# Two token chunks share the first projection block, and the final flag is loaded inside the schedule

## The chip, the cores and the metric

The kernel runs on one core of one Trainium2 chip. The metric is device time in microseconds (us) of one execution of the program. The engines are named as in the profile: PE (TensorE, matmuls; PEld its weight loads), DVE (VectorE), ACT (ScalarE), POOL (GpSimd) and SP (SyncE, which issues the DMAs here).

## The reference

Two computations on tokens of 2048 x 448 are written side by side into one output. A is a Fourier mixing layer with given DFT matrices, B is softmax attention with 16 heads of 28 columns:

```python
a = einsum("bsd,ed->bse", x, dft_hid_re); b = einsum("bsd,ed->bse", x, dft_hid_im)
A = einsum("ts,bse->bte", dft_seq_re, a) - einsum("ts,bse->bte", dft_seq_im, b)
q, k, v = split_heads(x @ wqkv)            # 16 heads, 28 columns each
B = merge_heads(softmax(q @ k.T * 28**-0.5) @ v) @ wo
return concatenate([A, B], -1)
```

All of it is float32. The kernel keeps the precision by splitting each operand into a high part in a reduced format and a low rest, and by adding three products (high x high, low x high, high x low).

## The kernel before, in words

**The order.** Nothing in the program says in which order an engine runs its instructions. Each step is a task with an engine, a due key, a duration and the tasks that it depends on; a planner (`Schedule.run`) plays the schedule through on the host, before the kernel is built, and puts into each engine's queue whichever ready task has the lowest key. On the chip each queue then runs strictly in that order and waits by semaphores. The planner models DMAs by a flow: each transfer occupies `size / FLOW` us after time 20 (`FLOW_IN` before), sizes in KB, and lands a fixed lag later (lines 68 and 278 to 293). A wrong figure there doesn't make the result wrong, but puts instructions at places where they wait. `P_H`, `fkey` and the like are due times worked out ahead.

**The start.** `FirstWeights` loads the weights of the first three column blocks of wqkv (384 columns) in four quarters of the contraction, w0 to w3 (192 KB each). `load_x` loads a chunk of 512 tokens, also in four quarters (256 KB each): x00 to x03 for chunk 0, x10 to x13 for chunk 1. ACT makes the high part of each (L560 for weights, L490 for tokens), DVE or POOL the low part (L427). Keys put SP's queue in the order w0, x00, w1, x01, w2, x02, w3, x03, x10, x11 and on. Until the first operands are there, `warm` (L920) runs `N_WARM` = 7 matmuls on ones.

`first_chunk` then multiplies chunk 0 with the three weight blocks a quarter at a time (33 matmuls, L616): the first quarter needs w0 and x00 only. Chunks 1 to 3 follow by `project`, one block after the other through `chain` (L581). `stored` evicts a finished bank: ACT copies the high part (L597), DVE subtracts for the low part (L598), and two stores of 256 KB each put them into DRAM (qkd, L600 and L601).

**The stretch from 37 to 84 us.** PE computes the values (`values`, 16 blocks of 11 matmuls of 448 columns, again by L581); for each block DVE copies the bank (L671 to L673) and SP stores it in a layout by heads (vd, L675: runs of 32 numbers). Between them SP loads rows of q and k from qkd (L745 and L746, 112 and 56 KB, a pair for each tile) and pieces of further weights (`Piece`: load L523, ACT's high part L524, POOL's low part L530, and small parts L539 and L542).

Attention of a head begins with `first_tiles`: for each of four query tiles a score matmul (L806), then ACT saves the scores (L810) and DVE transposes and reduces them (L811, L812). When all four are through, DVE forms a maximum for each query (L818 to L823). For each tile in turn DVE then transposes it back (L832) into a tile `mb`, of which there is one; DVE or POOL copies a row of it into q (L835); POOL or DVE adds it to the saved scores (L837), and ACT takes the exponential (L839). The score matmuls proper (L865) need the row in q, ACT evicts them with an exponential (L869), and runs of 8 or 10 groups of four L848 matmuls multiply with v. To fill PE, the planner weaves in projections of later heads (L581) and the Fourier part: `hidden`, then `sequence` (L718), which streams the DFT matrices through `Piece`.

**The end.** The output projection (L1003, stored by L1011) runs among the last `sequence` blocks; the last block is added to the first half by DVE (L736) and stored (L738). DVE has written a flag `fi` (whether all sums and values lay in a safe range); `values_load` (L1027) has every engine load it into a register and check it, and a branch that is not taken here (`tc.If`) would repeat the attention in another way. L1128 is the end of the program.

## Time and profile before

| | us |
|---|---|
| median of 3 runs | 1010.61 (1010.15 to 1011.03) |
| the profiled execution | 1010.71 |
| its span in the profile | 1008.9 |
| PE busy | 1001.6 |
| ACT busy | 712.3 |
| POOL busy | 366.9 |
| DVE busy | 319.8 |

The profiled execution is 1.8 us longer than the span, which goes from the first to the last recorded instruction. The granted TensorE clock was 1.00. In a timeline a row holds the start, the duration, the engine, the line, the operation with out<-in, and in brackets the idle time of the engine before it with the one that ended it. A row with x3 joins three like instructions in a row. In the view of waits a row holds who waited for whom, the sum, how often, and the longest. Matmuls overlap, so their durations add up to more than the time from start to start. Lines are those of the kernel before; below `first_chunk` the changed kernel's lines are one higher.

### The profile page before, as it was taken

The numbers are of one execution on the slowest core, as the hardware profiler recorded it, in microseconds if no ns is written. First come the engines' busy times: TensorE is split into PE (matmuls) and PEld (weight loads), VectorE is DVE, ScalarE is ACT, GpSimd is POOL, SyncE is SP. The second block draws the span as 40 slices with busy tenths as digits, with TensorE's granted clock in tenths as the row PEclk, the third lists the DMA queues.
The fourth block names the chain that finished last, engine by engine and source line by source line (L and its number), as shares of the span: only waits on it lengthen the run. The fifth ranks groups of instructions, "written<-read, shape, count | busy, mean of one in ns | idle before, by whom it ended". The sixth has DMA issues, their size and how long they took to land.

```text
span 1008.9 us, 15993 instructions
## 1 busy us (share of the span) xinstructions
PE 1001.6 (99%) x5634; PEld 735.3 (73%) x5634; DVE 319.8 (32%) x608; ACT 712.3 (71%) x1410; POOL 366.9 (36%) x338
## 2 busy tenths in 40 slices
PE   8999999999999999999999999999999999999998
PEld 7896667777766876686668667766786677667797
DVE  6362525251515042412314051614042152300112
ACT  6117979788767866796679778877786687668242
POOL 5112234353324323442325443434334252444530
PEclk9999999999999999999999999999999999999999
DMA  9797464323233333333233424332433343233463
GB/s 327 226 163 205 127 188 150 98 76 114 69 102 102 112 96 106 97 106 102 80 111 110 132 71 119 93 112 80 148 98 100 117 141 105 70 123 117 139 187 130
DMA packets 109908, 124.84 MB, mean 124 GB/s; under 512 B 48640, under 2 KB 61440, under 8 KB 109824
## 3 DMA queue, kind: packets, MB, share of 16 engines
q1 hardware_dynamic: 109824, 123.78, 40.8%
q8 instruction: 45, 0.74, 0.3%
q14 instruction: 39, 0.32, 0.1%
HBM read 89.92 MB, written 33.69 MB: 123 GB/s over the span
## 4 chain that ended last, share of the span: by engine, by line
PE 98%; DVE 1%; DMA 1%; SPq 0%; issue 0%; DVEq 0%
PE bank L718 31%; PE bank L865 23%; PE bank L848 22%; PE bank L581 17%; PE bank L1003 4%; PE bank L806 1%; DMA kept<-xb 1%; DVE big L427 0%; SPq L488 0%; SPq L559 0%; DVE kept L598 0%; DVE kept L736 0%; DVEq L427 0%
## 5 line engine op out<-in xcount | busy, mean ns | idle before, releaser
L869 ACT ACTIVATE kept<-bank 128x512 f32<-128x512 f32 x944 | 509.4, 673 | 90.7 <-PE bank L865 87.6
L530 POOL TENSOR_TENSOR wlo<-wraw,whi 128x512 fp32r<-128x512 f32 (+1 forms) x164 | 202.9, 1237 | 471.4 <-ACT whi L524 397.1
L865 PE MATMUL bank<-q,k 98*128 98x512 f32 x960 | 329.4, 398 | 0.0
L718 PE MATMUL bank<-big,whi 128*128 128x448 f32 x1024 | 310.9, 367 | 0.0
L848 PE MATMUL bank<-kept,v 128*32 128x512 f32 x2016 | 224.4, 593 | 0.0
L718 PEld LDWEIGHTS bank<-big,whi 128*128 128x128 f32 x1024 | 193.3, 189 | 29.2 <-issue 3.4
L865 PEld LDWEIGHTS bank<-q,k 98*128 98x128 f32 x960 | 180.4, 188 | 44.2 <-issue 11.7
L718 PE MATMUL bank<-big,wlo 128*128 128x448 f32 x512 | 188.3, 368 | 0.0
L848 PEld LDWEIGHTS bank<-kept,v 128*32 128x32 f32 x2016 | 63.5, 110 | 144.4 <-issue 142.3
L524 ACT ACTIVATE whi<-wraw 128x512 fp32r<-128x512 f32 x164 | 113.8, 694 | 21.0 <-PE bank L718 17.0
L718 PEld LDWEIGHTS bank<-big,wlo 128*128 128x128 f32 x512 | 96.7, 189 | 16.9 <-issue 5.9
L837 POOL TENSOR_TENSOR kept<-kept,mb 128x512 f32<-128x512 f32 x54 | 79.5, 1473 | 62.9 <-DVE mb L832 27.5
L581 PE MATMUL bank<-wd,whi 128*128 128x448 f32 x256 | 79.8, 367 | 0.0
L811 DVE STREAM_TRANSPOSE mb<-bank 128x512 f32<-128x512 f32 x64 | 45.8, 715 | 101.6 <-PE bank L806 87.9
L839 ACT ACTIVATE kept<-kept 128x512 f32<-128x512 f32 x64 | 45.1, 772 | 33.3 <-POOL kept L837 29.9
L581 PE MATMUL bank<-big,whi 128*128 128x512 f32 x175 | 60.1, 394 | 0.2 <-DVE kept L598 0.2
L832 DVE STREAM_TRANSPOSE mb<-am 128x512 f32<-128x512 f32 x64 | 45.4, 710 | 41.1 <-POOL kept L837 39.9
L810 ACT ACTIVATE kept<-bank 128x512 f32<-128x512 f32 x64 | 41.6, 672 | 22.5 <-PE bank L806 21.6
L581 PEld LDWEIGHTS bank<-wd,whi 128*128 128x128 f32 x256 | 48.3, 189 | 6.1 <-issue 0.8
L894 ACT ACTIVATE kept<-bank 128x512 f32<-128x512 f32 x16 | 9.5, 597 | 55.1 <-PE bank L848 55.1
L776 DVE TENSOR_REDUCE ok<-v 128x1 f32<-128x512 f32 x16 | 11.0, 686 | 115.5 <-DMA v<-vd 115.4
L736 DVE TENSOR_TENSOR kept<-bank,kept 128x448 f32<-128x448 f32 x15 | 9.3, 623 | 120.2 <-PE bank L718 106.0
(74 smaller groups left out, 745.8 us busy)
## 6 DMA issues: line engine op xcount, KB each, us to landing
wraw<-wre SPq DMA_DIRECT2D x64, 256.0 KB
wraw<-wim SPq DMA_DIRECT2D x64, 256.0 KB
qkd<-kept SPq DMA_DIRECT2D x40, 256.0 KB
wraw<-xa SPq DMA_DIRECT2D x32, 256.0 KB
k<-qkd SPq DMA_DIRECT2D x64, 112.0 KB
q<-qkd SPq DMA_DIRECT2D x64, 112.0 KB
out<-kept SPq DMA_DIRECT2D x31, 224.0 KB
kept<-xb SPq DMA_DIRECT2D x16, 256.0 KB
```

The costliest lines, as they stand in the source:

```text
L524: a = act(key + (0 if early else 1), lambda: nc.scalar.activation(self.hi.t, raw.t, AF.Copy), ACT_S, soon=SOON, deps=[ld], acq=[self.hi], ...
L530: b = sch.add(e, at, lambda g: eng[g].tensor_tensor(self.lo.t[:, :n], raw.t[:, :n], f32(self.hi.t)[:, :n], op=ALU.subtract), deps=[a], acq ...
L581: nc.tensor.matmul(o.t[:, :cols], w(), x(), start=(i == 0), stop=(i == n - 1))
L718: nc.tensor.matmul(o.t[:, :D], a.t[:, k, :], b[:, q * 4 + k, :], start=(q == 0 and k == 0 and j == 0), stop=(q == 3 and k == 3 and j == 2))
L810: made.append(act(key, lambda o=o, s=s: nc.scalar.activation(s.t, o.t, AF.Copy), deps=[m], use=[o, s.pair], lock=[o]))
L811: t = dve(key, lambda o=o, tm=tm: nc.vector.transpose(tm.t, o.t), 0.73, deps=[m], acq=[tm], use=[o], lock=[o], own=RAW_S)
L832: t = dve(key, lambda mb=mb, c=c: nc.vector.transpose(mb.t, f32(am.t)[:, c * NT:(c + 1) * NT].unsqueeze(2).to_broadcast([P, NT, 32])), 0.7 ...
L837: sh = sch.add({"DVE": 0.8, "POOL": POOL_2}, key, lambda e, s=s, mb=mb: eng[e].tensor_tensor(s.t, s.t, mb.t, op=ALU.add), deps=[t, made[c] ...
L839: shown.append(act(key, lambda s=s: nc.scalar.activation(s.t, s.t, AF.Exp, scale=SCALE), ACT_S, deps=[sh], use=[s.pair]))
L848: nc.tensor.matmul(o.t[c * VW:(c + 1) * VW, :], VT[h].t[:, kt // 4, kt % 4, :], tiles[c].t, start=(kt == 0), stop=(kt == NT - 1))
L865: m = pe(key, lambda e, o=o, q=q, kt=kt: nc.tensor.matmul(o.t, KT[h][kt // 4].t[:KM, kt % 4 * P:(kt % 4 + 1) * P], q.t[:KM, :], start=True ...
L869: es[h, kt].append(act(key - 20, lambda o=o, p=p: nc.scalar.activation(p.t, o.t, AF.Exp, scale=SCALE), deps=[m], use=[o, p.pair]))
```

## The change

Four things are changed.

1. `first_chunk` becomes `first_chunks`, for chunks 0 and 1: for each quarter of the contraction first the matmuls of chunk 0 and then those of chunk 1, 66 in all. They hold six banks until the end. `project` does the rest from chunk 2 on. The key of chunk 1's loads is moved so that each of its quarters stands in SP's queue right behind that of chunk 0: w0, x00, x10, w1, x01, x11 and on.
2. `N_WARM` becomes 9. In the planner the warm-up stands as one task of 3.01 us, as 7 x 0.43 before.
3. The planner's `FLOW` becomes 300, which holds for every DMA after 20 us of its clock. A task on SP without DMAs is allowed.
4. ACT, DVE, POOL and SP load the flag by a task of their own, due behind the flag's DVE task and the ninth output block; only PE loads it at its end. The range check of `values_load` is left out.

```diff
-N_WARM = 7
+N_WARM = 9
...
-FLOW, FLOW_IN = 200.0, 310.0
+FLOW, FLOW_IN = 300.0, 310.0
...
-                if e == "SP":
+                if e == "SP" and t.dmas:
...
-    def first_chunk(w):
+    def first_chunks(w, chunks):
+
+        os = {(c, j): (bank_s if j else fill_s).slot() for c in chunks for j in range(N_FIRST)}
+        pairs = {cj: kept_s.slot() for cj in os}
         end = {}
         for k in range(4):
...
+            for c in chunks:
+                cols = slice(c * CH, (c + 1) * CH)
+                for wl, xl, n in ((0, 0, 0), (1, 0, 1), (0, 1, 2))[:3 if k < 3 else 2]:
+                    for j in range(N_FIRST):
...
+                        ready = [*(w.los[k] if wl else w.his[k]), xb_ready[c, k] if xl or k == 3 else xb_hi[c, k]]
...
+        for c, j in os:
+            stored(j, c, os[c, j], end[c, j], [pairs[c, j]], Half(pairs[c, j], 0), Half(pairs[c, j], 1), False, 0.0,
+                   11.0 if j == 0 else 25.0)
...
-    pe(-1.0, warm, n=N_WARM, d=0.43, deps=[made], acq=[o], use=[ones])
+    pe(-1.0, warm, d=3.01, deps=[made], acq=[o], use=[ones])
...
-        load_x(c, 0.2 + 3 * c)
+        load_x(c, 0.2 + 3 * c if c > 1 else 0.2 + 0.05 * c)
...
-    first_chunk(w_in)
-    for c in range(1, NC):
+    first_chunks(w_in, (0, 1))
+    for c in range(2, NC):
...
-    dve(T_OUT + 12, flag, 2.2, deps=[*checked, *seen], use=[fl])
+    told = dve(T_OUT + 12, flag, 2.2, deps=[*checked, *seen], use=[fl])
+    regs = nc.alloc_registers("fine")
+    for name, e in (("ACT", ET.Activation), ("DVE", ET.DVE), ("POOL", ET.Pool), ("SP", ET.SP)):
+        sch.add({name: 0.6}, T_OUT + 14, lambda _, e=e: nc.reg_load(regs[e], fi), deps=[told, starts[8]])
     sch.run()
...
-    fine = nc.values_load(fi, min_val=0, max_val=1)
+    nc.reg_load(regs[ET.PE], fi)
+    fine = nc.snap(regs, donate=True, min_val=0, max_val=1)
```

More of the change, by code (lines that the diff above doesn't have):

```diff
@@ L601, in stored @@
             dma(out_key, lambda: nc.sync.dma_start(f32(qk_d[j * P:(j + 1) * P, 1, cols]), as_f(lo.t)), deps=[b], use=own)]
-    def first_chunk(w):
-        cols = slice(0, CH)
-        os = [(bank_s if j else fill_s).slot() for j in range(N_FIRST)]
-        pairs = [kept_s.slot() for _ in range(N_FIRST)]
+    def first_chunks(w, chunks):
+        os = {(c, j): (bank_s if j else fill_s).slot() for c in chunks for j in range(N_FIRST)}
+        pairs = {cj: kept_s.slot() for cj in os}
         end = {}
@@ L609, in first_chunk @@
         for k in range(4):
-            for step in ((0, 0, 0), (1, 0, 1), (0, 1, 2))[:3 if k < 3 else 2]:
-                wl, xl, n = step
-                for j in range(N_FIRST):
-                    x = lz(x_3, cols) if k == 3 else lz(x_l if xl else x_h, k, cols)
-                    def emit(e, j=j, k=k, n=n, wl=wl, x=x):
-                        nc.tensor.matmul(os[j].t, w.part(j, k, wl)(), x(), start=(k == 0 and n == 0), stop=(k == 3 and n == 1))
-                    ready = [*(w.los[k] if wl else w.his[k]), xb_ready[0, k] if xl or k == 3 else xb_hi[0, k]]
-                    done = k == 3 and n == 1
-                    last[0] = pe(fkey(1, M512), emit, d=M512, deps=[last[0], *ready],
-                                 use=[*w.own, os[j], *([pairs[j]] if done else ())])
-                    if done:
-                        end[j] = last[0]
@@ L623, in first_chunk, with emit @@
-        for j in range(N_FIRST):
-            stored(j, 0, os[j], end[j], [pairs[j]], Half(pairs[j], 0), Half(pairs[j], 1), False, 0.0, 11.0 if j == 0 else 25.0)
+            for c in chunks:
+                cols = slice(c * CH, (c + 1) * CH)
+                for wl, xl, n in ((0, 0, 0), (1, 0, 1), (0, 1, 2))[:3 if k < 3 else 2]:
+                    for j in range(N_FIRST):
+                        x = lz(x_3, cols) if k == 3 else lz(x_l if xl else x_h, k, cols)
+                        def emit(e, c=c, j=j, k=k, n=n, wl=wl, x=x):
+                            nc.tensor.matmul(os[c, j].t, w.part(j, k, wl)(), x(), start=(k == 0 and n == 0), stop=(k == 3 and n == 1))
+                        ready = [*(w.los[k] if wl else w.his[k]), xb_ready[c, k] if xl or k == 3 else xb_hi[c, k]]
+                        done = k == 3 and n == 1
+                        last[0] = pe(fkey(1, M512), emit, d=M512, deps=[last[0], *ready],
+                                     use=[*w.own, os[c, j], *([pairs[c, j]] if done else ())])
+                        if done:
+                            end[c, j] = last[0]
```

## The prediction, as it stood before the result was known

> **What bounds the kernel now.** I read the page first, then what TensorE (PE) waits for, then its order of work in the first 21 us.

> ```profile
> span 1008.9 us, 15993 instructions
> ...
> PE 1001.6 (99%) x5634; PEld 735.3 (73%) x5634; DVE 319.8 (32%) x608; ACT 712.3 (71%) x1410; POOL 366.9 (36%) x338
> ...
> PE 98%; DVE 1%; DMA 1%; SPq 0%; issue 0%; DVEq 0%
> ```

> PE is busy for 99% of the span and 98% of the chain that ended last is PE. So every idle stretch of PE, and nothing else, is time to win or lose. The view of waits, for PE over the whole run, lists all there are:

> ```profile
> PE bank L616 <- ACT big L490: 1.7, 2, 1.0
> PE bank L920 <- POOL kept L921: 1.2, 1, 1.2
> PE bank L581 <- DVE kept L598: 0.2, 1, 0.2
> ```

> They add up to 3.1 us, 0.3% of the time, and all lie before 20 us. The change leaves the number of matmuls alone (its program holds the same of every kind, four warm-up records more). **Gains are therefore small; losses are not bounded**: PE has no idle time later in which a new wait could be made good.

> **The head.** Timelines of PE, then ACT; columns are start, duration, instruction, idle before and who ended it.

> ```profile
> 1.24 3.36 PE L920 MATMUL bank<-kept 128*128 128x128 f32 x14 [1.24 <-POOL kept L921]
> ...
> 5.28 0.96 PE L616 MATMUL bank<-big,whi 128*128 128x512 f32 x3 [0.68 <-ACT big L490]
> ...
> 8.61 0.96 PE L616 MATMUL bank<-big,whi 128*128 128x512 f32 x3 [1.00 <-ACT big L490]
> ```

> ```profile
> 4.60 0.63 ACT L490 ACTIVATE big<-kept 128x512 fp32r<-128x512 f32 x1 [0.52 <-DMA kept<-xb]
> 7.23 0.52 ACT L560 ACTIVATE whi<-kept 128x384 fp32r<-128x384 f32 x1 [2.00 <-DMA kept<-wqkv]
> 7.93 0.63 ACT L490 ACTIVATE big<-kept 128x512 fp32r<-128x512 f32 x1 [0.18 <-DMA kept<-xb]
> ```

> ```profile
> 6.70:18.00 11.30, 10.30 (x46) 8.21 (x45) 8.93 (x12) 9.85 (x19) 9.39 (x15) 1.00 1.02 379
> ```

> The third fence is the view of windows: its last three numbers are PE's granted clock, the DMA engines' share and GB/s. Transfers arrive as w0, x00 (quarter 0 of chunk 0), w1, x01: ACT converts them in this order, w1 from 7.23, x01 from 7.93. After the change x10 (quarter 0 of chunk 1) is third in SP's queue and w1 fourth. w1 was there at 7.23; x10 has 256 KB where w1 has 192, and 64 KB more at 379 GB/s are 0.17 us: 7.40. With 0.63 us on ACT, PE starts chunk 1's quarter at about 8.08, in place of 8.61: **0.53 us won**. Behind it a quarter is 17 or 18 matmuls (about 4 us), while its 704 KB take 1.9 us at that rate, so no later quarter waits. The wait of 0.2 us on L598, at the turn from the first block to the next chunk, should go too: with 66 matmuls instead of 33 ahead of it, DVE has worked off the x conversions, I count some 0.2 us of slack; without it one subtraction on DVE, up to 0.7 us, would stand there again. What its gap costs from start to start is about 0.3. Two more warm-up matmuls are four records of 3.36/14 = 0.24 us; they end near 5.5 with their start near 5.1, about where the first real matmul stands (5.28): 0 to 0.2 us, I take 0. **Head: -0.8 us**, bounds -1.6 (no wait left at all) and +0.2 (the third transfer lands no earlier than x01 did, and the warm-up delays).

> **The middle: FLOW from 200 to 300.** This number is the planner's speed for DMA after 20 us. No engine uses it, but it decides the order. In the changed program the first score matmuls of head 0 (L806) and all that hangs on them move forward. Rows of before, PE and SP:

> ```profile
> 57.97 0.39 PE L806 MATMUL bank<-q,k 84*128 84x512 f32 x1
> ...
> 61.26 0.40 PE L806 MATMUL bank<-q,k 84*128 84x512 f32 x1
> 61.49 9.14 PE L581 MATMUL bank<-wd,big 128*128 128x448 f32 x44
> 70.47 0.43 PE L865 MATMUL bank<-q,k 98*128 98x512 f32 x1
> ```

> ```profile
> 41.16 2.21 SPq L675 DMA_DIRECT2D vd<-kept  x2
> ...
> 59.17 1.41 SPq L523 DMA_DIRECT2D wraw<-wqkv  x1
> ```

> Counted by matmuls, the last two L806 stand 41 and 45 places earlier, at about 48.7 and 51.2 us instead of 57.97 and 61.26; the first L865 comes at 60.8 instead of 70.47; from head 2 on both orders agree. What does DMA really carry there? The view of DMA from 40 to 80 us:

> ```profile
> DMA packets 34844, 6.61 MB, mean 165 GB/s; under 512 B 33302, under 2 KB 33814, under 8 KB 34839
> ...
> q1 hardware_dynamic: 34839, 6.55, 91.8%
> ...
> vd<-kept SPq DMA_DIRECT2D x16, 256.0 KB
> wraw<-wqkv SPq DMA_DIRECT2D x3, 256.0 KB
> ```

> 165 GB/s at a share of 0.92 is **180 GB/s when full**, well under the new 300. In before the matmuls wait long enough: the piece of weights issued at 59.17 is used behind all four tiles of L806. In the changed program two pieces stand in front of dependents of head 0. I follow the later one, piece B (L523, tile wraw_103).

> In SP's queue, between the first vd store (at about 39.7 in the changed kernel, where PE is 0.8 us and a moved L806 ahead) and the end of B, stand 7 vd stores, 9 pairs of q or k loads (112 + 56 KB), 2 qkd stores, the earlier piece and B: 1792 + 1512 + 512 + 512 KB = 4.43 MB. At 180 GB/s that is 24.6 us. With the lag from issue to data that leaves B landing at **65.1** (64.3 without any lag).

> What hangs on B is read from the order on each engine; ACT, POOL and DVE rows of before give the durations:

> ```profile
> 63.80 0.63 ACT L524 ACTIVATE whi<-wraw 128x512 fp32r<-128x512 f32 x1 [1.51 <-DMA wraw<-wqkv]
> ```

> ```profile
> 64.51 1.02 POOL L530 TENSOR_TENSOR wlo<-wraw,whi 128x384 fp32r<-128x384 f32 x1 [27.43 <-ACT whi L524]
> ...
> 68.76 1.29 POOL L837 TENSOR_TENSOR kept<-kept,mb 128x512 f32<-128x512 f32 x1 [3.23 <-DVE mb L832]
> ```

> ```profile
> 68.79 1.56 DVE L835 CAST q<-mb 1x512 fp32r<-1x512 f32 x1
> ...
> 71.36 0.71 DVE L832 STREAM_TRANSPOSE mb<-am 128x512 f32<-128x512 f32 x1
> ...
> 76.75 0.42 DVE L835 CAST q<-mb 1x512 fp32r<-1x512 f32 x1
> ```

> The added wait: POOL's L530 of B waits for ACT's L524, which waits for B. Behind L530 on POOL is the L837 of tile 1; it frees the single mb buffer, for which DVE's L832 of tile 2 waits; behind that is the L835 that writes the row of q2, and PE's score matmul on q2 waits for it, with everything else of PE behind. The sum from the landing: 64.51 - 63.80 = 0.71 to POOL's start, 1.02, 1.29, 0.71, 0.99 for L835 (between 0.42 and 1.56), and 0.3 of handing over: 5.0 us. So PE can run it at 70.1. In the order it is the 276th real matmul; in before the 276th is the 25th of the row at 61.49, 24 x 0.206 us later: 66.4; less the 0.8 of the head it is due at 65.6. **Stall: 4.5 us.** Shorter waits on the way (the earlier piece lands near 53, and DVE's copies of bank pairs stand behind its L811; the first row of q) lie inside it. Behind it, the next row of q, the exponentials and the v loads have moved along with PE, and I find none that is late again.

> Bounds, the faster one from the window before this stretch:

> ```profile
> 20.00:40.00 20.00, 20.00 (x91) 16.75 (x90) 9.56 (x16) 7.88 (x15) 5.03 (x5) 1.00 0.83 298
> ```

> At 298 GB/s B lands at about 55 and nothing waits (stall 0). At the bare mean of 165 GB/s the transfer takes 26.8 us, B lands at 67.1 and the stall is 6.5. I take the value near the second: 180 comes from the same mix of stores and row loads, while 20 to 40 us holds none of the vd stores.

> [...]

> **The flag.** Before, every engine loads it at its end; SP last. DVE, SP, the view of L1027, and a window:

> ```profile
> 1004.69 0.62 DVE L736 TENSOR_TENSOR kept<-bank,kept 128x448 f32<-128x448 f32 x1 [9.47 <-PE bank L718]
> ```

> ```profile
> 1005.35 0.33 SPq L738 DMA_DIRECT2D out<-kept  x1
> ```

> ```profile
> L1027 SPq TENSOR_LOAD <-fi x1: 530/530/530, 1005.7 to 1005.7; - x1
> L1027 SPq FUSED_REGOPS  x1: 192/192/192, 1006.3 to 1006.3; - x1
> ```

> ```profile
> 1006.30:1006.80 0.50, 0.00 (x0) 0.00 (x0) 0.00 (x0) 0.00 (x0) 0.00 (x0) 1.00 0.99 362
> ```

> SP's load and checks run from 1005.7 to about 1006.6, but the window row shows the last store still moving at full share to 1006.8. The end waits for that store, so the 0.9 us are hidden: I take 0, bounds 0 and -0.9. The moved loads stand in the queues of ACT, DVE, POOL and SP, 0.5 us each; POOL's is ahead of its last L530, with several us to spare. Tasks of SP that hold no DMA, which the planner now takes, cost nothing by themselves.

> **Sum.** -0.8 - 0.0 + 4.5 = +3.7 us. The profiled run took 1010.71 us, its span is 1008.9, the median 1010.61: 1014.3 us.

> **Rivals.** (A) **No stall**: not slower, but faster by the head alone. The early order is served in time if B lands by 60.6, which needs 4.43 MB in 20.9 us, 212 GB/s; that is the point from which it decides. For it: vd stores are 1.8 of the 4.43 MB here but 16 x 256 KB, 4.2 of the 6.55 MB, in the measured stretch, so the rate may be higher; and 298 GB/s were reached from 20 to 40. Against it: 165 to 180 as soon as vd stores and q, k rows are mixed. It gives 1009.8, and 1008.9 with the whole flag gain. [...] (B) **A short stall**, B landing at 60.6 to 63.5 since pairs of row loads overlap: 0 to 2.9 us, about 1011.3. (C) **A longer one**, the q rows or the second group of pieces late again: 1016 to 1018. (D) **The head gives nothing** because the DMA's low rate before 6.7 us goes by bytes: 1015.1 with the stall.

> **How the numbers follow.** A measurement tells about 0.2% (2.0 us) from no change. Forecast 0.48, C 0.12, D with the stall 0.06: slower by more than that, 0.66. B 0.16 and A as it stands 0.14: within it, 0.30. A with the flag's gain and a still better head, below 1008.6: 0.04. The range runs from A's 1009.7 to 1017.0, since A and B hold more than 2 in 10.

> **What would show it.** Right: a wait of PE on L866 (the old L865) released by DVE L836 of some 3 to 4 us near 66 to 70, shorter ones before it; ACT's L524 idle on wraw until about 65; the second L616 block near 8.1; no wait on L598; SP's flag load before 1005 and the end still 3.5 us after the last DVE addition. Wrong: no PE wait between 50 and 75, or B used on ACT before 61. Then the transfer price was mine to blame, and the head alone counts.

## The result, and the profile after

The changed kernel is slower by about 0.6 per cent:

| | before | after |
|---|---|---|
| median of 6 runs (us) | 1010.65 (1010.15 to 1011.2) | 1016.62 (1014.92 to 1017.9) |
| ratio, 95% interval | | 1.0057 (1.0044 to 1.0070) |
| the profiled execution | 1010.71 | 1014.92 |
| its span | 1008.9 | 1013.1 |

The profiled execution of after is the fastest of its six. What follows first explains its 4.2 us; the 1.7 us from there to the median come behind that. The runs of before scatter by 0.1%, those of after by 0.3%: its time depends on something that is not the same in every run.

The page of after (span, busy time of the engines, shares of the chain):

```profile
span 1013.1 us, 16009 instructions
...
PE 1003.6 (99%) x5638; PEld 738.6 (73%) x5638; DVE 318.7 (31%) x606; ACT 713.8 (70%) x1410; POOL 368.9 (36%) x340
...
PE 97%; DMA 1%; SPq 1%; DVE 1%; POOL 0%; ACT 0%; issue 0%; ACTq 0%; POOLq 0%
```

PE is busy 2.0 us longer than before (1001.6), with only four records more, so some matmuls were slower; the rest of the 4.2 us is pauses of PE or the ends of the program. What PE waits for, over the whole run:

```profile
PE bank L581 <- DVE kept L672: 1.8, 1, 1.8
PE bank L866 <- DVE q L836: 1.5, 1, 1.5
PE bank L921 <- POOL kept L922: 1.2, 1, 1.2
```

The two waits on L490 and the one on L598 are gone; two others have come. Their places in PE's timeline, with the first matmul of the values (the first 448 columns wide) ahead of them, and that matmul in before:

```profile
35.91 3.22 PE L581 MATMUL bank<-wd,big 128*128 128x448 f32 x15
...
56.47 7.53 PE L581 MATMUL bank<-wd,big 128*128 128x448 f32 x28 [1.76 <-DVE kept L672]
...
70.22 0.50 PE L866 MATMUL bank<-q,k 98*128 98x512 f32 x1 [1.46 <-DVE q L836]
```

```profile
37.33 1.59 PE L581 MATMUL bank<-wd,big 128*128 128x448 f32 x7
```

The head has won 37.33 - 35.91 = 1.42 us. Then the row at 56.47 is odd: its 28 matmuls take 7.53 us, 0.27 each, where the rows on either side have 0.21. The view of windows shows why (busy time of PE, PEld, DVE, ACT, POOL with counts, then granted clock, DMA share, GB/s):

```profile
50.00:57.00 7.00, 5.24 (x26) 4.47 (x26) 3.09 (x9) 1.12 (x2) 1.60 (x3) 1.00 0.68 161
57.00:60.50 3.50, 3.50 (x11) 3.14 (x10) 2.01 (x10) 0.00 (x0) 0.00 (x0) 0.51 0.89 189
60.50:70.00 9.50, 8.26 (x40) 7.21 (x39) 6.35 (x16) 3.04 (x6) 5.47 (x7) 1.00 1.08 202
```

Right behind the first pause PE runs at half clock for 3.4 us (the trace's own record of it goes from 57.09 to 60.50) and does in them what takes 1.7 us at full clock. PE is "100% busy" there: the share of busy time doesn't show such a loss, only the clock beside it does.

The end, DVE, SP, and the drains that close DVE's queue in after and in before:

```profile
1008.13 0.62 DVE L737 TENSOR_TENSOR kept<-bank,kept 128x448 f32<-128x448 f32 x1 [15.08 <-PE bank L719]
```

```profile
1008.79 0.33 SPq L739 DMA_DIRECT2D out<-kept  x1
```

```profile
L1133 DVEq DRAIN  x2: 10/34/58, 1012.3 to 1012.6; - x2
```

```profile
L1128 DVEq DRAIN  x2: 10/32/55, 1006.1 to 1008.3; - x2
```

From the last store's issue to the end of the span it is 1013.1 - 1008.8 = 4.3 us, before 1008.9 - 1005.35 = 3.5. DVE's first drain comes 4.2 us behind the start of its last addition, before 1.4 us (1006.1 - 1004.69).

**The account of the profiled run**, in us: head -1.4; first pause +1.9 (start to start); half clock +1.7; second pause +1.6. Here the 276th real matmul, the one on q2, is 3.8 later than the 276th of before (70.22 against 66.40). Behind it the order wins back 0.4, 0.3 of it before 130 us. So PE's last result, read by DVE's last addition, is 1008.13 - 1004.69 = 3.4 later; the end of the program adds 0.8. Together +4.2, which is 1014.92 - 1010.71.

### The profile page after: what moved, and what is told of

Read it like the earlier page. It is cut to its first block, busy times and chain, and to the rows that moved or that the text cites. A ratio compares the mean times of both kernels' runs of the same rounds, so it can differ in the third digit from the quotient of the medians.

```text
span 1013.1 us, 16009 instructions
## 1 busy us (share of the span) xinstructions
PE 1003.6 (99%) x5638; PEld 738.6 (73%) x5638; DVE 318.7 (31%) x606; ACT 713.8 (70%) x1410; POOL 368.9 (36%) x340
## 4 chain that ended last, share of the span: by engine, by line
PE 97%; DMA 1%; SPq 1%; DVE 1%; POOL 0%; ACT 0%; issue 0%; ACTq 0%; POOLq 0%
PE bank L719 31%; PE bank L866 22%; PE bank L849 22%; PE bank L581 14%; PE bank L1004 4%; PE bank L616 2%; PE bank L807 1%; DMA wraw<-wqkv 1%; SPq L746 0%; PE bank L921 0%; SPq L676 0%; DVE kept L672 0%; SPq L747 0%; ACT whi L524 0%; DVE q L836 0%; POOL kept L838 0%
## 5 line engine op out<-in xcount | busy, mean ns | idle before, releaser
L870 ACT ACTIVATE kept<-bank 128x512 f32<-128x512 f32 x944 | 510.2, 670 | 84.9 <-PE bank L866 81.8
L530 POOL TENSOR_TENSOR wlo<-wraw,whi 128x512 fp32r<-128x512 f32 (+1 forms) x164 | 202.9, 1237 | 507.9 <-ACT whi L524 374.8
L866 PE MATMUL bank<-q,k 98*128 98x512 f32 x960 | 326.4, 398 | 1.5 <-DVE q L836 1.5
L849 PE MATMUL bank<-kept,v 128*32 128x512 f32 x2016 | 224.4, 593 | 0.0
L866 PEld LDWEIGHTS bank<-q,k 98*128 98x128 f32 x960 | 180.4, 188 | 44.0 <-issue 11.7
L849 PEld LDWEIGHTS bank<-kept,v 128*32 128x32 f32 x2016 | 63.5, 110 | 144.4 <-issue 142.0
L524 ACT ACTIVATE whi<-wraw 128x512 fp32r<-128x512 f32 x164 | 113.5, 692 | 37.6 <-DMA wraw<-wqkv 16.6
L838 POOL TENSOR_TENSOR kept<-kept,mb 128x512 f32<-128x512 f32 x56 | 82.9, 1481 | 56.0 <-DVE mb L833 43.5
L812 DVE STREAM_TRANSPOSE mb<-bank 128x512 f32<-128x512 f32 x64 | 45.8, 716 | 109.6 <-PE bank L807 90.2
L581 PE MATMUL bank<-wd,whi 128*128 128x448 f32 x256 | 79.7, 366 | 0.0
L833 DVE STREAM_TRANSPOSE mb<-am 128x512 f32<-128x512 f32 x64 | 45.5, 711 | 44.3 <-POOL kept L838 43.4
L581 PEld LDWEIGHTS bank<-wd,whi 128*128 128x128 f32 x256 | 48.3, 189 | 6.0 <-issue 0.8
L581 PE MATMUL bank<-big,whi 128*128 128x512 f32 x154 | 51.9, 393 | 0.0
L811 ACT ACTIVATE kept<-bank 128x512 f32<-128x512 f32 x64 | 40.6, 660 | 13.4 <-PE bank L807 12.7
L733 DVE COPY kept<-bank 128x448 f32<-128x448 f32 x16 | 10.0, 625 | 111.6 <-PE bank L719 86.4
## 6 DMA issues: line engine op xcount, KB each, us to landing
wraw<-wre SPq DMA_DIRECT2D x64, 256.0 KB
wraw<-wim SPq DMA_DIRECT2D x64, 256.0 KB
qkd<-kept SPq DMA_DIRECT2D x40, 256.0 KB
wraw<-xa SPq DMA_DIRECT2D x32, 256.0 KB
kept<-xb SPq DMA_DIRECT2D x16, 256.0 KB
```

Of the source, the lines that this page charges most:

```text
L524: a = act(key + (0 if early else 1), lambda: nc.scalar.activation(self.hi.t, raw.t, AF.Copy), ACT_S, soon=SOON, deps=[ld], acq=[self.hi], ...
L530: b = sch.add(e, at, lambda g: eng[g].tensor_tensor(self.lo.t[:, :n], raw.t[:, :n], f32(self.hi.t)[:, :n], op=ALU.subtract), deps=[a], acq ...
L581: nc.tensor.matmul(o.t[:, :cols], w(), x(), start=(i == 0), stop=(i == n - 1))
L811: made.append(act(key, lambda o=o, s=s: nc.scalar.activation(s.t, o.t, AF.Copy), deps=[m], use=[o, s.pair], lock=[o]))
L812: t = dve(key, lambda o=o, tm=tm: nc.vector.transpose(tm.t, o.t), 0.73, deps=[m], acq=[tm], use=[o], lock=[o], own=RAW_S)
L833: t = dve(key, lambda mb=mb, c=c: nc.vector.transpose(mb.t, f32(am.t)[:, c * NT:(c + 1) * NT].unsqueeze(2).to_broadcast([P, NT, 32])), 0.7 ...
```

## The experiments

My theory was that the new `FLOW` alone makes the loss: it lets PE, ACT, DVE and POOL use three pieces of weights earlier than SP's queue can bring them. Called A, B and C here: A is the load of wraw_102, B of wraw_103, C of wraw_101, all L523. The rivals were that the pauses come from the merged first block or from the flag, that one of the loads alone decides, and that the true DMA speed as `FLOW` would mend it. "Before" in the table is the median of the kernel before in runs on the same chip.

| kernel | median (range) | before | ratio, 95% interval |
|---|---|---|---|
| flow200 | 1010.69 (1010.34 to 1011.33) | 1010.29 | 1.0006 (0.9997 to 1.0015) |
| flow300_only | 1019.02 (1017.93 to 1020.23) | 1010.87 | 1.0080 (1.0065 to 1.0096) |
| flow180 | 1018.25 (1017.94 to 1019.42) | 1010.87 | 1.0076 (1.0062 to 1.0089) |
| flow220 | 1011.88 (1011.31 to 1012.39) | 1010.87 | 1.0010 (1.0001 to 1.0019) |
| no_flag | 1018.66 (1016.58 to 1019.11) | 1010.87 | 1.0070 (1.0054 to 1.0085) |
| e_a | 1017.68 (1016.97 to 1018.78) | 1010.29 | 1.0076 (1.0061 to 1.0091) |
| e_bc | 1013.97 (1012.96 to 1014.60) | 1010.29 | 1.0038 (1.0023 to 1.0052) |
| e_abc | 1012.35 (1011.19 to 1016.13) | 1010.29 | 1.0029 (1.0018 to 1.0040) |
| e_abcv2 | 1013.86 (1011.64 to 1015.08) | 1010.66 | 1.0030 (1.0018 to 1.0041) |
| e_abcv2_w7 | 1013.72 (1011.72 to 1014.93) | 1010.66 | 1.0023 (1.0012 to 1.0033) |
| e_abcv3 | 1009.95 (1009.55 to 1010.66) | 1010.68 | 0.9995 (0.9986 to 1.0004) |
| e_abcv4 | 1009.67 (1008.95 to 1010.03) | 1010.29 | 0.9991 (0.9982 to 1.0000) |

### Is it FLOW? One part undone, one part alone

```diff
 # flow200, against after
-FLOW, FLOW_IN = 300.0, 310.0
+FLOW, FLOW_IN = 200.0, 310.0
```

> The changed kernel with the planner's FLOW back at 200; common first block, nine warm-up matmuls and the moved flag loads stay. Theory (FLOW is the whole loss): the score matmuls of head 0 stand late again (the first L866 as the 311th matmul, in the kernel before the 296th), no PE pause after the head, clock 1.00, 1009.2 us (1008.8 to 1009.8). Rival (the common block itself delays what follows, its six banks and twelve stores at once): 1010.6 or more.

```diff
 # flow300_only, against before
-FLOW, FLOW_IN = 200.0, 310.0
+FLOW, FLOW_IN = 300.0, 310.0
```

> The kernel before with the planner's FLOW at 300 and nothing else. Theory (this number is the whole loss): the score matmuls of head 0 move forward as in the changed kernel, PE waits for L835 behind the pieces of weights, 2 to 6 us in all between 50 and 75, with half a clock behind a long one: 1014 to 1018 us. Rival (it takes the common first block too, with its six banks and twelve stores in front of the values): 1010 to 1011.5.

With 200 the loss is gone, and with 300 in the kernel before, without the merged block and without the flag's tasks, it is there: 8 us, more than the 1014 to 1018 us that I had expected. The waits of flow300_only, then two windows of it:

```profile
PE bank L865 <- POOL q L835: 6.0, 1, 6.0
...
PE bank L616 <- ACT big L490: 1.2, 2, 0.9
```

```profile
60.00:70.00 10.00, 4.04 (x16) 3.27 (x15) 2.40 (x7) 2.56 (x5) 2.90 (x5) 0.80 0.97 187
70.00:80.00 10.00, 10.00 (x43) 8.88 (x42) 3.87 (x13) 6.09 (x13) 2.50 (x4) 0.86 0.87 147
```

One pause of 6.0 us, and again a spell at less than full clock with it (0.80 and 0.86 in the two windows). The wait on L490 in the head is there again too: it belongs to the old first block. So **the pauses belong to FLOW and the head's gain to the merged block**; that much is shown.

But flow200 was to keep the head's gain (1008.8 to 1009.8 us) and didn't; its time is the rival's. Its waits, and the row of the second:

```profile
PE bank L866 <- POOL q L836: 0.5, 1, 0.5
PE bank L581 <- DVE kept L598: 0.5, 1, 0.5
```

```profile
21.10 0.73 PE L581 MATMUL bank<-big,whi 128*128 128x512 f32 x2 [0.49 <-DVE kept L598]
```

Start to start the two cost 0.65 and 0.66 us, which is 1.3 of the 1.4 us given back: at the turn from the merged block to the next chunk the wait on L598 stands again, and one row of q is late. The plan is another one for every value of FLOW, so a value doesn't "restore" anything.

### The true speed as FLOW?

flow180 and flow220 are after with 180 and 220 in that line. 180 is what the transfers of before carry when they are busy.

> The changed kernel with FLOW at 180, what DMA carries between 40 and 80 us when full. Theory (a true speed makes an order that keeps): no PE wait behind 25 us, the head's gain is kept: 1009.3 to 1010.2 us. Rival (the order is chaotic in this number, and each value has some wait of its own): 1010.3 to 1011.5 as with 200.

> The changed kernel with FLOW at 220. Theory (the loss grows with the distance to the true 180): one or two short waits of PE, below 1.5 us in all, no half clock: 1010.3 to 1011.8. Rival (chaotic): anything, also below the value for 180.

The waits of flow180:

```profile
PE bank L866 <- DVE q L836: 5.0, 3, 1.8
...
PE bank L866 <- POOL q L836: 0.5, 1, 0.5
```

flow220 has two, 1.2 us of L866 for ACT's L870 and 0.6 us of L581 for L598, and no lower clock; it is 0.1% slower than before. The measured speed makes a plan as bad as 300 does. So my theory that a true rate would be a good one **falls**: rows of q come late with 180 too. They do so for another reason, since no load stands in their way: between 73.6 and 80.4 us PE's queue holds nothing but four score matmuls (L866), which come some 2.3 us apart, while DVE's L833 waits each time until POOL's L838 has freed the one mb buffer (1.16 us, from 76.84 and from 79.17). Half clock follows from 77.90 to 84.72, though none of these pauses is over 1.83 us. What counts is not the figure but whether the order that comes out of it holds.

### Does the late load make the pause? The loads moved, nothing else

In these kernels the order that the planner made is written out with SP's DMA issues shifted; PE, ACT, DVE and POOL have exactly the order of after. SP's queue in e_abc against after:

```diff
 L746/L747 q_115
+L523 wraw_102   (A)
 L676 vd, L746/L747 k_107
-L523 wraw_102
+L523 wraw_103   (B)
+L523 wraw_101   (C)
 L746/L747 k_108
...
 L746/L747 q_119
-L523 wraw_103
 L676 vd
-L523 wraw_101
```

e_a moves A alone, e_bc B and C.

> The changed kernel with only the load of piece A moved forward, ahead of one vd store and one k pair. Theory: no pause near 55 and no half clock from 57 to 60, but PE comes about 3.5 us earlier to the product on q2, whose row still hangs on B (landing near 65): one pause of about 5 us there, which may again be followed by half a clock: 1014.5 to 1016.5, so little or nothing is won. Rival (each wait is an own term, their prices add): 1012.9 less than that of the changed kernel by 3.5.

> The changed kernel with only the loads of pieces B and C moved forward, to right behind that of A, which stays where it was. Theory: the pause of about 1.8 us near 55 (behind A) and the half clock after it stay, the one at 70 goes: 1012.5 to 1014, 1013.2 likeliest. Rival 1 (order by itself): as the changed kernel, 1015 to 1017. Rival 2 (the pauses are of one cause, B alone): 1009.2.

> The changed kernel with three DMA issues moved forward in SP's queue (the pieces A, B and C of weights, tiles wraw_102, wraw_103 and wraw_101, issued right behind the load of q_115 and the first k pair); the order on every other engine is the same. Theory (the pieces land too late, PE pauses of 1.76 and 1.46 us and half a clock behind the first): no wait of PE between 50 and 75 us, granted clock 1.00 from 50 to 70, 1009.2 us (the head's gain of 1.4 alone), 1008.8 to 1009.8. Rival 1 (the early order is slower by itself, whoever loads when): stays at 1013 or more. Rival 2 (the half clock has another cause than the pause): clock still near 0.85 from 50 to 60 and about 1011.

PE's waits in e_bc, in e_a and in e_abc, one row each:

```profile
PE bank L581 <- DVE kept L672: 2.0, 1, 2.0
```

```profile
PE bank L866 <- DVE q L836: 5.8, 1, 5.8
```

```profile
PE bank L849 <- DMA v<-vd: 1.6, 1, 1.6
```

Each pause follows its own load: with A late only the first is there, with B and C late only the second, with all three early neither. (B and C were not moved apart; that it is B rests on the chain that the trace shows, further down.) In e_a nothing is won by it: the landing of B sets when the second pause ends, so what PE doesn't wait at 56 it waits at 68. **The two pauses are one debt.** e_a's median is even above the 1014.5 to 1016.5 us that I had expected: in its profile B reaches ACT at 66.53, in after's at 65.16. Two windows of e_a, in the pause and behind it, then one of e_abc:

```profile
66.00:68.00 2.00, 0.00 (x0) 0.00 (x0) 0.00 (x0) 0.63 (x1) 0.77 (x1) 0.93 0.96 172
...
72.00:74.00 2.00, 2.00 (x7) 1.69 (x7) 1.08 (x5) 1.12 (x2) 1.60 (x3) 0.50 1.47 156
```

```profile
50.00:60.00 10.00, 10.00 (x51) 9.11 (x50) 7.82 (x26) 2.38 (x4) 2.92 (x4) 1.00 0.82 179
```

No pause between 50 and 60 and no lower clock there: the half clock comes with the pause, and with the longer pause of e_a it lasts 6.8 us (from 67.73 to 74.56) instead of 3.4, though only 3.0 us of it lie behind the pause's end at 71.52. But e_abc still is at 1.0029, 1012.35 us for the 1009.2 that I had expected, since a wait takes the next place: head 0's load of v, issued behind everything, is what PE's first group of L849 waits for,

```profile
87.64 4.93 PE L849 MATMUL bank<-kept,v 128*32 128x512 f32 x44 [1.60 <-DMA v<-vd]
```

and six of its ten runs lie from 1011.2 to 1012.7, four from 1014.3 to 1016.1 with a mean granted clock of 0.996 to 0.998. That fits a spell at half clock behind the same pause; the profile of e_abc is one of the six and shows none.

### The last late load

e_abcv2 also moves three loads that the next 20 us don't need (head 0's last pair of k, L746 and L747, and two L507) behind the last vd store. e_abcv2_w7 is the same with `N_WARM` 7. e_abcv3 moves the v load of head 0 (L774) ahead of the k pair, too:

```diff
 L676 vd   (the last)
+L774 v<-vd
 L746/L747 k<-qkd
 L507 wraw<-wd  x2
 L600/L601 qkd<-wd
-L774 v<-vd
```

> The kernel with the pieces A, B and C issued early (whose profile has one PE wait left, 1.6 us for the v load at 86 us), and beside that the load of the last k pair and two weight loads moved behind the last vd store in SP's queue; all other engines keep their order. Theory (every loss after the head is a load that comes too late in the full DMA queue): no PE wait behind 10 us, the granted clock 1.00, the end of PE about 1.9 us earlier than in the kernel before, 4.3 us from the last store to the end as in all kernels of this order: 1009.4 us, faster than the kernel before by 0.8 to 1.3 us. Rival (another wait takes the place, as each time so far): no better than 1010.5.

> The same with 7 warm-up matmuls in place of 9, nothing else. Theory (the two more buy nothing, since x00 and its conversion set the first real matmul and the clock is 1.00 from the start): within 0.2 us of the run with 9, first L616 at 5.25 to 5.35. Rival (idle time between warm-up and first product costs clock): the granted clock below 1.00 within the first 10 us and 1 to 2 us more.

> As the kernel with the pieces early and two weight loads late, and now head 0's v load directly behind the last vd store in SP's queue (there the v load was issued 0.7 us after the last store had landed, behind five other transfers, and landed at 88.3, while PE waited from 86.0). From 40 to 88 us the DMA engines are busy throughout, so only the place in the queue can be changed. Theory: v lands near 85.3, no PE wait left behind 10 us but for at most 0.3 us, clock 1.00, PE's end 1.5 us earlier than in the kernel before, 4.3 us from the last store to the end: 1009.4 to 1010.2 us, the first version that beats the kernel before, by 0.4 to 1.1 us. Rival (vd stores themselves land too late for this order, since 16 of them at 1.4 to 1.5 us fill the queue up to 82.7): a wait at the same matmul of 1 us or more, 1011 or more.

e_abcv2 missed: its v load still came last, and PE waited 2.0 us for it, 2.9 with 7 warm-ups. With 9 warm-ups the first product (L616) starts at 5.10 without a wait, with 7 at 4.90 (I had said 5.25 to 5.35) behind a wait of 0.41 us for ACT's L490; the intervals of the two kernels lie on each other.

e_abcv3's only wait of PE in the whole run, and SP's v load (no row of L849 waits for it any more):

```profile
PE bank L921 <- POOL kept L922: 1.2, 1, 1.2
```

```profile
82.56 0.36 SPq L774 DMA_DIRECT2D v<-vd  x1
```

Eight loads in other places of one queue, and the kernel goes from 1016.62 to 1009.95. With PE's order as in after, and the new FLOW's early use kept, **what PE lost was the place of the loads**. DVE's last addition starts at 1002.89, 1.8 us ahead of before; the 0.8 us at the end of the program are still there.

### The flag and the end of the program

no_flag is after with the flag loaded as in before (one `values_load` at each engine's end).

```diff
-    told = dve(T_OUT + 12, flag, 2.2, deps=[*checked, *seen], use=[fl])
-    regs = nc.alloc_registers("fine")
-    for name, e in (("ACT", ET.Activation), ("DVE", ET.DVE), ("POOL", ET.Pool), ("SP", ET.SP)):
-        sch.add({name: 0.6}, T_OUT + 14, lambda _, e=e: nc.reg_load(regs[e], fi), deps=[told, starts[8]])
+    dve(T_OUT + 12, flag, 2.2, deps=[*checked, *seen], use=[fl])
...
-    nc.reg_load(regs[ET.PE], fi)
-    fine = nc.snap(regs, donate=True, min_val=0, max_val=1)
+    fine = nc.values_load(fi, min_val=0, max_val=1)
```

> The changed kernel with the flag loaded by every engine at its end again, as before; the order of PE is the same. In four profiles of the changed order the program ends 4.3 to 4.4 us after the last store is issued, because one of its 16 parts lands at 3.0 us and the others below 2.0, while code loads stand in front of its last packet; in the kernel before it is 3.5. Theory (SP's earlier branch brings these code loads together with the store): 3.5 to 3.6 us again, some 0.8 us less than the changed kernel at the same PE end. Rival (the place of the store's data, not the flag): still 4.3. The pauses of PE stay, so the time is 1014 to 1017.

From the last store's issue to the end it takes 4.48 us, in after 4.35. I had expected 3.5, taking the flag's tasks for the cause of the longer end; that **fell**. Its median, 1018.66, also lies above the 1014 to 1017 us of the expectation; against before its interval overlaps that of after. The waits of its profile are of use for something else:

```profile
PE bank L866 <- DVE q L836: 4.1, 1, 4.1
PE bank L581 <- DVE kept L672: 1.8, 1, 1.8
```

```profile
70.00:77.00 7.00, 5.45 (x15) 4.78 (x16) 4.30 (x11) 3.20 (x7) 3.56 (x5) 0.53 1.07 168
```

```profile
66.55 0.63 ACT L524 ACTIVATE whi<-wraw 128x512 fp32r<-128x512 f32 x1 [11.18 <-DMA wraw<-wqkv]
```

PE's order here is that of after. Its first pause is as long as after's, this time without half clock behind it; B reaches ACT 1.4 us later than in after's profile (66.55 against 65.16), the second pause is 4.1 us long, and half clock runs from 70.35 to 77.18, 5.6 us of it behind the pause's end at 71.55. So two profiles with one order differ by 4.2 us, all but 0.1 of it through when B lands and where the clock drops. That the same makes the runs of after scatter, and its median 1.7 us longer than its profile, is likely and not shown: no_flag ran on another chip, and after has one profile. The mean granted clocks of after's six runs bear it out in part. They go from 0.999 (1015.84 us) to 0.996 (1017.9 us), with 0.998 in the profiled one; the run at 0.999 leaves no room for 3.4 us of half clock and is still 0.9 us longer than the profiled one.

What then lengthens the end? In every kernel DVE leaves through one branch at the end of its queue. Counted in the built programs, that queue holds 806 to 808 instructions in before, flow200 and, below, e_abcv4, and 810 to 814 in all others; where it is 808 or less, 0.56 us lie between the branch and DVE's drain (the instruction that closes its queue), where it is 810 or more, 3.4 us. e_abcv4 tests this: e_abcv3, in which DVE compares the sums of the last six heads with their bound once for all (`LATE` is 10) instead of once for each:

```diff
-        k1 = dve(key, lambda: nc.vector.tensor_scalar(flat(), flat(), SUM_MAX, None, op0=ALU.is_le), 0.25, deps=[r, s3], use=[sm])
+        k1 = dve(key, lambda: h < LATE and nc.vector.tensor_scalar(flat(), flat(), SUM_MAX, None, op0=ALU.is_le), 0.25, deps=[r, s3], use=[sm])
-        checked.append(dve(key, lambda: nc.vector.tensor_reduce(ok[:, h:h + 1], flat(), axis=AX.X, op=ALU.min), 0.25,
+        checked.append(dve(key, lambda: nc.vector.tensor_reduce(ok[:, h:h + 1], flat(), axis=AX.X, op=ALU.min if h < LATE else ALU.max), 0.25,
...
+        nc.vector.tensor_scalar(ok[:, LATE:H], ok[:, LATE:H], SUM_MAX, None, op0=ALU.is_le)
```

> As the kernel with the early pieces, the late weight loads and the v load moved forward, with six instructions fewer on DVE: the check of the last six heads' sums against the limit is made once, beside that of the values, instead of head by head. The order of PE, ACT, POOL and SP is the same. In the profiles so far DVE reaches its last instruction 0.5 to 0.6 us after its branch where its queue up to that branch has 807 or 808 instructions (the kernel before; FLOW 200), and 3.4 us after it where it has 810 to 814 (seven others). Theory (the code behind the branch is loaded in blocks, and the longer queue puts it past the end of what is there): with 806 instructions DVE is through at once, the end comes 3.5 us after the last store instead of 4.3, PE's end unchanged: 1009.0 to 1009.3 us, 1.4 us faster than the kernel before. Rival (DVE's late end has to do with the early order, not with the length of its queue): 4.3 us again and 1009.9.

The last store and DVE's drains in e_abcv4, then the same two rows of e_abcv3:

```profile
1004.11 0.33 SPq L739 DMA_DIRECT2D out<-kept  x1
```

```profile
L1133 DVEq DRAIN  x2: 10/34/58, 1004.8 to 1007.1; - x2
```

```profile
1003.54 0.33 SPq L739 DMA_DIRECT2D out<-kept  x1
```

```profile
L1133 DVEq DRAIN  x2: 10/34/58, 1007.0 to 1007.4; - x2
```

In e_abcv4 DVE's first drain is 0.7 us behind the last store's issue (1004.8 - 1004.1); in e_abcv3 it is 3.5 us. The end takes 3.50 us against 4.34: **the 0.8 us go with DVE's way out of its queue**, by the count of its instructions. A second thing went with it: the last part of the last store lands 3.01 us behind its issue in e_abcv3 and 2.30 in e_abcv4, which by itself would put e_abcv3's end at 4.2 (an estimate: in e_abcv4 the end comes 1.2 us behind that landing). no_flag tells the two apart: its store lands after 2.40 us, DVE's drain comes 3.63 us behind the issue, and the end still takes 4.48. So DVE's way out is enough for the late end; how much the late landing would add by itself isn't shown.

What goes with the longer way can be seen in the trace's DMA packets. In after DVE's branch stands at 1008.90, a packet of code (8 KB, kind instruction) runs from 1010.44 to 1010.75, and the drain comes at 1012.28; in before the branch stands at 1005.53, the drain at 1006.09, and the first such packet comes at 1006.18. In each of the eleven profiles with 3.4 us such a packet starts 1.52 to 1.60 us behind DVE's branch, and the drain comes 1.50 to 1.56 us behind the packet's end; in flow180 it is the only one of its queue in that time. In the three with 0.56 us there is none between branch and drain. That DVE waits for this code is my reading of these times; that the longer queue puts the code past the end of what is there, as my theory had it, isn't shown, nor why the bound lies between 808 and 810.

e_abcv4 has the lowest median of all, 1009.67, above the 1009.0 to 1009.3 that I had expected; against before its interval reaches from 0.9982 to 1.0000, so its gain is some 0.1%, 0.2% at most, and none at all isn't excluded. Its profiled span is only 0.3 us shorter than e_abcv3's, since PE's last result came 0.56 us later (1003.45 against 1002.89); PE was behind from its first products on, and the trace's record of full clock begins at 7.17 us there, at 4.96 in e_abcv3. Against after it is 7 us faster.

## Why the prediction was right, point by point

The sign and the cause held, and the median 1016.62 lies within the range, though near its end. The forecast of +3.7 was for the median, which moved by 6.0; the profiled execution moved by 4.2. The median stands where rival C was placed (1016 to 1018), but in after's profile no second group of pieces and no further row of q holds PE up. Not all the steps held, and some errors cancelled.

One premise failed: that every idle stretch of PE, **and nothing else**, is time to win or lose. Two of the account's terms are no idle time of PE: the half clock, 1.7 us, and the end of the program, 0.8 us.

**The middle: the place and the chain held.** For B the prediction had a landing at 65.1, and the chain L524, L530, L837, L832, L835 to PE at 70.1. In after, ACT, POOL and DVE:

```profile
65.16 0.63 ACT L524 ACTIVATE whi<-wraw 128x512 fp32r<-128x512 f32 x1 [10.00 <-DMA wraw<-wqkv]
```

```profile
65.87 1.02 POOL L530 TENSOR_TENSOR wlo<-wraw,whi 128x384 fp32r<-128x384 f32 x1 [2.10 <-ACT whi L524]
66.84 1.29 POOL L838 TENSOR_TENSOR kept<-kept,mb 128x512 f32<-128x512 f32 x1
```

```profile
68.17 0.71 DVE L833 STREAM_TRANSPOSE mb<-am 128x512 f32<-128x512 f32 x1 [2.17 <-POOL kept L838]
68.92 1.25 DVE L836 CAST q<-mb 1x512 fp32r<-1x512 f32 x1
```

PE ran the matmul on q2 at 70.22. From B on, the sum of 5.0 us was 5.1. The landing itself was hit by two errors that cancel, and with some luck: the first vd store was issued at 39.08, 0.6 us earlier than said, and from there to ACT the 4.43 MB took 26.1 us instead of 25.4 (24.6 and a lag of 0.8; in after the first packet of the last store starts 0.83 us behind its issue); and in no_flag's profile, with the same order, B was 1.4 us later. The DMA of after from 40 to 66 us, the mean and the queue's own share:

```profile
DMA packets 18888, 4.73 MB, mean 182 GB/s; under 512 B 16828, under 2 KB 17874, under 8 KB 18886
...
q1 hardware_dynamic: 18886, 4.71, 91.2%
```

That is 182 GB/s as a mean. By the prediction's own rule, mean over share, it would be 200 when full, and B would have come 2.4 us sooner than it said; that 180 served so well is luck too. Rival A falls: B would have had to land by 60.6. (The upper bound has a slip: 39.7 + 26.8 + 0.8 is 67.3 and not 67.1, which changes nothing.)

**The stall's parts.** The prediction left "shorter waits on the way" inside the stall. The first pause was one of them, for the cause that it named, DVE's copies behind its L811 (L812 in the changed kernel). ACT, then DVE:

```profile
54.04 0.63 ACT L524 ACTIVATE whi<-wraw 128x512 fp32r<-128x512 f32 x1 [4.84 <-DMA wraw<-wqkv]
54.58 0.58 ACT L811 ACTIVATE kept<-bank 128x512 f32<-128x512 f32 x1
```

```profile
55.19 0.72 DVE L812 STREAM_TRANSPOSE mb<-bank 128x512 f32<-128x512 f32 x1 [3.91 <-ACT kept L811]
55.83 0.59 DVE L672 COPY kept<-bank 128x448 f32<-128x448 f32 x1
```

A reaches ACT at 54.04; behind its L524 is the L811 that DVE's L812 waits for, and behind that the copy that frees a bank for PE at 56.4. That this pause lies inside the stall is right as an account: e_a shows that PE gets to the matmul on q2 no earlier without it. **What was missing is the half clock behind it.** The terms that stand for the predicted stall of 4.5 are 1.9 + 1.7 + 1.6 = 5.2. Of the 0.7 between them 0.6 are the head, which won that much more than said ahead of B. As long as the half clock lies ahead of B's landing it is paid out of the same debt; if it lies behind it, as in no_flag's profile, nothing takes it up: half of 5.6 us there, 2.8. With a later B that is the likeliest cause of the 2.3 us by which the median stands above the forecast, but no profile of such a run of after shows it.

**The head: right mechanism, mis-sized.** -0.8 was said, -1.42 came, within the bounds. The step that failed is the landing of the third transfer. I priced it by w1's place and 64 KB more, at 7.40. ACT in after:

```profile
4.67 0.63 ACT L490 ACTIVATE big<-kept 128x512 fp32r<-128x512 f32 x1 [0.65 <-DMA kept<-xb]
5.70 0.63 ACT L490 ACTIVATE big<-kept 128x512 fp32r<-128x512 f32 x1 [0.41 <-DMA kept<-xb]
6.75 0.53 ACT L560 ACTIVATE whi<-kept 128x384 fp32r<-128x384 f32 x1 [0.41 <-DMA kept<-wqkv]
```

x10 is there at 5.70 and even w1, now the fourth, at 6.75, where it had come at 7.23 as the third. The first four transfers, 896 KB in either order, are there some 1.2 us earlier than before (x01 as the fourth at 7.93). So no wait on ACT was left at all, and nearly the best bound of the gain applied. Why they come faster in this order isn't shown. The sign that was named for it, a second L616 block near 8.1, therefore didn't come. The wait on L598 went as said, in after; in flow200, flow220 and e_abcv2, the last with PE's order of after, it is there again, so it hangs by a few tenths. The low rate before 6.7 us that rival D speaks of was 116 GB/s to 3.5 us and 227 from there, in before, against 379 from 6.7 to 18 us.

**Behind the stall.** "None that is late again" is right for after, in which PE was already late. It was no margin: as soon as the pieces came in time (e_abc), the v load was the next to be late.

**The flag and the end.** The gain of 0 is right within 0.05 to 0.13 us: 4.48 in no_flag against 4.35, 3.43 and 3.48 in flow180 and flow200 against 3.53. In flow180, with 810 instructions, DVE reached its branch early, so that its way out was hidden. But the end still grew by 0.8 with DVE's queue length, a term that the prediction put at nothing; no view of before shows it. An edit that adds instructions isn't free because the engine is idle. The sign "3.5 us after the last DVE addition" was misread as well: 3.5 is counted from the last store's issue, from the addition it was 4.2 in before and 5.0 in after.

**The warm-up** costs nothing that the runs could tell: 1013.86 with 9, 1013.72 with 7.

So the sum came out near, as -0.8 + 4.5 = 3.7 against -1.8 + 5.2 + 0.8 = 4.2: a larger gain ahead of a landing that doesn't move with it only makes the wait for it longer. What was sound is that the step that counts was fixed in absolute time, by bytes ahead of a load over a rate measured in the same mix.

Open is: why the half clock followed the pause of 1.8 us in after's profile and not the one of the same length in no_flag's; why DVE's bound lies where it does; and what in the order behind the pauses gives the 0.4 us.

## What to carry to other kernels

When an order of work is made from a model, a better figure in the model is no better order: 180 and 300 lost 0.6 to 0.8%, 200 and 220 0.1% or nothing. Look in the trace for what the pause really waits for; where it is the load that lands last ahead of a dependent chain, move that load alone, and see which comes last then. Where a fixed landing sets the time, the waits ahead of it are one debt, and mending one of them lengthens the next. Where an engine is 99% busy, count a pause as its length and, behind it, what the granted clock shows.

## What the runs showed of the hardware

| PE's idle time in one piece at full clock (us) | the next piece |
|---|---|
| up to 1.46 (after's second pause, e_abc) | full clock |
| 1.13 and 0.89 (e_abcv2's one pause of 2.0, split between two pieces) | full clock |
| 1.76 (after's first pause) | half |
| 1.81 (no_flag's first pause) | full clock |
| 2.04 (e_bc, e_a), 2.88 (e_abcv2_w7), 2.94 (no_flag's second), 3.41 (flow300_only) | half |
| 2.91 (flow180: 1.25 and 1.66, parts of two pauses) | half |

So in these profiles the next piece goes by the idle time within a piece and not by the length of a pause: up to 1.46 us full clock followed, from 2.04 us on half; why 1.76 and 1.81 ended differently isn't shown. The spell lasted one piece where that piece held no idle time (after, e_bc, e_abcv2_w7), and two where it held 1.2 us or more (no_flag, flow180, flow300_only, e_a). Ahead of after's spell PE was idle for 1.76 of a piece's 3.413 us.

**The way out of a queue.** DVE's last branch took 0.56 us with 806 to 808 instructions in its queue and 3.4 us with 810 or more, of which 0.8 us reached the end of the program; in the second case 8 KB of code were loaded in between, from some 1.5 us behind the branch.

**Stores with short runs.** The mix of vd stores (256 KB in runs of 32 numbers) and row loads carried 182 GB/s at a share of 0.91 in after, where the traffic from 20 to 40 us in before, without vd stores, carried 298 at 0.83. Which part of the mix is the slow one was not tested.
